# A three-stage token kernel on one core: the first block's filter matrix is fetched another way, the last block's arithmetic is dealt out to other engines, and the planner's table is new

## The chip, the cores and the metric

The program runs on 1 core of a Trainium2 chip. The core has TensorE (PE, matrix products into PSUM), VectorE (DVE), ScalarE (ACT), GpSimd (POOL, which here works on SBUF tiles alone) and SyncE (SP, which here only issues DMAs). The metric is the device time of one execution in microseconds; lower is better.

## The reference, cut to what matters

Everything is float32. 8192 tokens (2 sequences of 4096) of 192 numbers pass through three stages, and the last result is the output.

```
w   = softmax(weight, axis=-1)                     # 8 heads x 7 taps
out = einsum('hk,bskhg->bshg', w, windows(x, 7))   # causal: 6 zero rows ahead of a sequence, 24 channels a head
h   = out @ moe_w_in ; g = maximum(0.01 * h, h)    # 192 -> 2048
y   = g @ moe_w_out                                # 2048 -> 192
h   = y @ moe2_w_in
P   = a0 + a1*h + a2*h^2 + a3*h^3
Q   = 1 + |b0|*|h| + |b1|*h^2
z   = (P / (Q + 1e-6)) @ moe2_w_out
```

The four weight matrices arrive as 64-bit floats, so the kernel reads them as pairs of 32-bit words and turns them into float32 itself.

## The kernel before, in words

**Blocks and groups.** The tokens are cut into 16 blocks of 512. The 2048 hidden columns are cut into 16 groups of 128 (`j`). For one layer, block and group, PE runs `gemm1` (five matmuls of 128x512 into one PSUM bank), other engines make the activation `g` from it, split it into a rounded part `gH` and a remainder `gL`, and PE runs `gemm2_hi` (three matmuls with `gH`) and `gemm2_lo` (two with `gL`), which add into two accumulator banks. The three-part products carry float32 accuracy through a faster matmul format.

**Per group of layer 2.** ACT makes `p1 = a3*h + a2` and `|b1|*|h|` (`l2_vp`, two instructions); DVE makes `D = (|b1||h| + |b0|)*h` (`l2_D`); ACT takes its absolute value (`l2_abs`), then `1/sqrt(D + 1)` and its square (`l2_rs`, `l2_R`), and `D + 1` (`l2_Q`, on ACT or POOL as the planner picks). DVE makes the polynomial (`l2_p2`, `l2_p3`) and `gH` (`l2_hi`). POOL multiplies `Q * gH` (`l2_w`), DVE takes the remainder (`l2_r`), POOL multiplies it by `R` into `gL` (`l2_lo`). That is five DVE instructions, six or seven of ACT and two or three of POOL for ten matmuls. Layer 1 needs one of DVE, two of ACT and one of POOL per group.

**The first stage.** The causal filter is a matmul: the taps of a head stand along the diagonals of a 109x103 band matrix, the moving operand holds the rows of `x` in chunks of 103 tokens, and PE's result is copied by ACT (`conv_evac`) to `xc`, transposed by PE (`trans`) and split by ACT and DVE (`x_hi`, `x_lo`). To make the band, the softmaxed taps are put into a DRAM scratch (`s_put`, ACT's queue), read back twice with a stride of one element a partition (`s_get`, ACT's queue, 256 KB each), and turned round in the free dimension by DVE (first half) and ACT (second half) (`s_band`).

**The start.** Weights come in pieces (`raw` buffers, three of them) on SP's queue. A piece is made into float32 by two ACT and four DVE instructions (`cv_abs`, `cv_low`, `cv_clip`, `cv_bits`) and split (`w_hi` ACT, `w_lo` DVE or POOL). A piece of kind `r` is first copied to both partition halves by DMA (`r_dup`). PE runs 11 matmuls without use ahead of the first filter (`s_warm`) and one after the filter and one after the transposes (`s_fill`).

**What sets the order.** `Planner.run` lays out all groups of instructions before the program is built. Each has a rank (a base plus `OFF[name]`) and an estimated duration; among those whose inputs are there and which lie within `WINDOW` of the lowest rank and among the first `LOOK` of an engine, it takes the one with the least start plus `PULL * rank`. Each engine then runs its instructions strictly in that order, so one that waits holds all behind it. Layer 2 of a block is interleaved with layer 1 of the block two further on; only the end of the program has layer 2 alone. In the profile L234 is any ACT arithmetic, L237 and L240 the two-input forms on DVE or POOL, L243 a matmul, L474 a transpose of `trans`, L323 `s_get`, L329 `s_band` on DVE, L411 `r_dup`, L619 the stores of the output.

## Time and profile before

| | us |
|---|---|
| median of 3 runs (lowest, highest) | 1282.11 (1279.03, 1282.89) |
| the profiled execution | 1279.76 |
| its span in the trace | 1278.0 |
| PE busy in the span | 1238.8 (97%) |
| ACT, DVE, POOL busy | 1183.0, 1171.2, 1145.9 |

The span begins with the first instruction and ends with the last; 1.76 us of the execution lie outside it. Four engines are busy 90% of it or more, so an average tells little. The page's 40 slices show where that is not so: the first slice and the last two. The rest of the reading goes by stretches.

### The profile page before, as it was taken

The page shows a single profiled execution, that of the slowest core. Times are in us where ns is not written, and L with a number is a line of the kernel's source. Part 1 is how long each engine was busy: PE and PEld are TensorE (multiplying, and loading weights), DVE is VectorE, ACT ScalarE, POOL GpSimd, SP SyncE. Part 2 cuts the span into 40 slices and gives each one's busy share as a digit, 9 for nine tenths or more (in the row PEclk, how much of TensorE's full clock was granted, in tenths as well). Part 3 has the DMA queues.
Part 4 walks back from the last instruction along what each step waited for, and adds up shares of the span by engine and source line. Part 5 has one row for each costly group of instructions (what it writes and reads, how often), then busy time and mean ns, then how long its engine had stood idle before and what let it go on. Part 6 is the DMA issues. An engine that isn't in the chain of part 4 may idle for free.

```text
span 1278.0 us, 17949 instructions
## 1 busy us (share of the span) xinstructions
PE 1238.8 (97%) x5562; PEld 1005.1 (79%) x5562; DVE 1171.2 (92%) x1797; ACT 1183.0 (93%) x2193; POOL 1145.9 (90%) x922
## 2 busy tenths in 40 slices
PE   7999999999999999999999999999999999999975
PEld 5777878888888788887878878788888888888753
DVE  5999989999998989989899999999999989999997
ACT  5999999999999999999989999999999999999995
POOL 1896999999999899998989899999999999989886
PEclk8999999999999999999999999999999999999998
DMA  6551001010010101000000101001010100000000
GB/s 180 140 176 57 1 1 28 1 29 1 1 28 1 27 1 28 1 8 21 1 13 1 28 1 20 9 1 28 1 28 1 29 1 7 7 1 13 1 13 13
DMA packets 70140, 30.21 MB, mean 24 GB/s; under 512 B 52518, under 2 KB 67484, under 8 KB 70044
## 3 DMA queue, kind: packets, MB, share of 16 engines
q1 hardware_dynamic: 68956, 28.54, 9.0%
q8 instruction: 43, 0.70, 0.2%
q10 hardware_dynamic: 1088, 0.53, 0.1%
q14 instruction: 53, 0.43, 0.1%
HBM read 20.67 MB, written 6.30 MB: 21 GB/s over the span
## 4 chain that ended last, share of the span: by engine, by line
PE 75%; DVE 12%; ACT 8%; issue 2%; POOL 1%; DMA 1%; ACTq 0%; DVEq 0%; POOLq 0%
PE bank L243 39%; PE acc L243 36%; ACT work L234 4%; DVE work L237 2%; DVE work L240 2%; DVE bank L240 2%; ACT raw L234 2%; DVE pair L240 2%; DVE raw L240 1%; DVE xl L237 1%; ACT pair L234 1%; PE bank L474 1%; ACT xh L234 1%; POOL pair L237 1%; DVE bank L376 1%
## 5 line engine op out<-in xcount | busy, mean ns | idle before, releaser
L243 PE MATMUL acc<-pair,wo 128*128 128x512 f32 x2560 | 655.9, 393 | 7.7 <-POOL pair L237 6.9
L243 PEld LDWEIGHTS acc<-pair,wo 128*128 128x128 f32 x2560 | 478.8, 189 | 110.0 <-POOL pair L237 10.1
L234 ACT ACTIVATE work<-work 128x512 f32<-128x512 f32 x550 | 339.2, 634 | 23.0 <-DVE work L240 18.9
L237 POOL TENSOR_TENSOR pair<-work,pair 128x512 fp32r<-128x512 f32 x192 | 249.8, 1303 | 29.2 <-ACT pair L234 26.7
L237 DVE TENSOR_TENSOR work<-work,bank 128x512 f32<-128x512 f32 x364 | 243.5, 678 | 7.2 <-ACT work L234 6.5
L237 POOL TENSOR_TENSOR work<-work,pair 128x512 f32<-128x512 f32 x156 | 202.4, 1297 | 37.2 <-DVE pair L240 20.2
L243 PE MATMUL bank<-xh,wiH 128*128 128x512 f32 x512 | 208.2, 407 | 16.5 <-DVE work L240 6.4
L234 ACT ACTIVATE work<-bank 128x512 f32<-128x512 f32 x348 | 205.0, 595 | 8.5 <-PE bank L243 6.8
L243 PE MATMUL bank<-xh,wiL 128*128 128x512 f32 x512 | 200.5, 392 | 1.2 <-POOL wiL L237 1.2
L243 PE MATMUL bank<-xh,wiR 128*128 128x512 f32 x512 | 200.3, 391 | 0.3 <-DVE wiR L237 0.3
L243 PE MATMUL bank<-xl,wiH 128*128 128x512 f32 x512 | 200.2, 391 | 0.0
L243 PE MATMUL bank<-xl,wiR 128*128 128x512 f32 x512 | 200.0, 391 | 0.0
L234 ACT ACTIVATE raw<-raw 128x512 f32<-128x512 f32 x242 | 149.4, 633 | 9.5 <-DVE raw L240 8.4
L237 POOL TENSOR_TENSOR raw<-raw,pair 128x512 f32<-128x512 f32 x100 | 130.3, 1303 | 21.0 <-DVE pair L240 13.1
L240 DVE SCALAR_TENSOR_TENSOR pair<-bank,a_sb,work 128x512 fp32r<-128x512 f32 x192 | 142.7, 743 | 6.3 <-PE acc L243 2.5
L237 POOL TENSOR_TENSOR pair<-work,work 128x512 fp32r<-128x512 f32 x112 | 145.5, 1301 | 3.2 <-DVE work L240 2.3
L243 PEld LDWEIGHTS bank<-xh,wiH 128*128 128x128 f32 x512 | 96.3, 188 | 58.9 <-DVE work L240 15.7
L240 DVE SCALAR_TENSOR_TENSOR work<-work,b_sb,bank 128x512 f32<-128x512 f32 x156 | 115.4, 740 | 18.0 <-ACT work L234 16.8
L240 DVE SCALAR_TENSOR_TENSOR bank<-work,a_sb,bank 128x512 f32<-128x512 f32 x172 | 128.8, 749 | 2.1
L240 DVE SCALAR_TENSOR_TENSOR work<-bank,a_sb,work 128x512 f32<-128x512 f32 x156 | 116.3, 745 | 14.4 <-POOL work L237 13.3
L234 ACT ACTIVATE pair<-work 128x512 fp32r<-128x512 f32 x192 | 121.3, 633 | 2.2 <-DVE work L237 1.5
L234 ACT ACTIVATE work<-bank,a_sb 128x512 f32<-128x512 f32 x172 | 117.3, 682 | 4.3 <-PE bank L243 2.4
(81 smaller groups left out, 1896.9 us busy)
## 6 DMA issues: line engine op xcount, KB each, us to landing
raw<-in_moe_w_out_dram SPq DMA_DIRECT2D x16, 384.0 KB, 3.2
xt<-in_x_dram SPq DMA_DIRECT2D x14, 384.0 KB, 3.6
out_dram<-work SPq DMA_DIRECT2D x80, 64.0 KB, 1.9
raw<-in_moe_w_in_dram SPq DMA_DIRECT2D x8, 512.0 KB
raw<-in_moe_w_in_dram SPq DMA_DIRECT2D x8, 256.0 KB, 4.4
work<-work SPq DMA_DIRECT2D x16, 128.0 KB, 2.7
xt<-in_x_dram SPq DMA_DIRECT2D x18, 72.0 KB, 3.8
out_dram<-raw SPq DMA_DIRECT2D x16, 64.0 KB, 2.8
```

Source lines behind the costliest of these rows:

```text
L234: nc.scalar.activation(out=out_, in_=in_, func=func, **k)
L237: (eng or nc.vector).tensor_tensor(out=out_, in0=in0, in1=in1, op=op)
L240: nc.vector.scalar_tensor_tensor(out=out_, in0=in0, scalar=s, in1=in1, op0=op0, op1=op1)
L243: nc.tensor.matmul(out=out_, lhsT=w, rhs=r, start=start, stop=stop)
L376: nc.vector.tensor_scalar(out=a, in0=a, scalar1=F64_TINY, scalar2=F64_HUGE, op0=ALU.max, op1=ALU.min)
L474: nc.tensor.transpose(ps[:, t * CT:t * CT + k], xc[0:k, t, m * P:(m + 1) * P], ident[0:k, 0:k])
```

## The change

- The band is read back straight into its tile, both halves on SP's queue, and nobody turns it round (`s_get`; `s_band` is gone). The filter's results of a chunk therefore come out with the tokens reversed; `trans` writes the chunks from the back of its bank, so that a whole block is reversed, and `x_hi` and `x_lo` of layer 1 read the bank backwards. The last chunk of a block is loaded with 109 rows instead of 106, and the stationary operand is the last 103 columns of the band.
- SP reads the small vectors `a`, `b` after the band, and the third weight piece (`w_out`) only once the first is converted.
- For the first block the wrapped columns of `xc` are copied by DVE (`conv_wrap`) instead of ACT.
- PE gets 13 useless matmuls at the start instead of 11, one more behind the first block's `x_lo`, and four that wait for the first `w_out` piece (`FEED0`).
- In the last block, groups 2, 5, 8 and 11 make `D` without DVE: ACT takes `|h|` and `|b1|*|h|+|b0|` and POOL multiplies them (`l2_up`, `l2_t`, `l2_ut`). The planner may put `l2_lo` of groups 14 and 15 and `l2_w` of group 15 on DVE. `gemm2_hi` of groups 13 to 15 may come before their `gemm2_lo`s, which come last, together; four useless matmuls (`FEED`) wait for tiles of groups 13 to 15. Three of the six last stores go out on ACT's queue.
- The planner's numbers differ: `GAP`, `PREP`, `WINDOW`, `LOOK`, `REST`, `FIN`, `CV2`, `CV3` and 14 entries of `OFF`.

```diff
-PREP = 27.404
-WARM = 11
+PREP = 26.968
+WARM = 13
-WINDOW = 27.767
-LOOK = 19
+WINDOW = 39.292
+LOOK = 28
-CV1, CV2, CV3 = 9.735, 23.683, 5.167
+CV1, CV2, CV3 = 9.735, 28.752, 4.82
+FEED0 = ((('xl', 0, 0, 0), 1), (('wH', 0, 'o', 0), 2), (('wL', 0, 'o', 0), 2))
+GPDEN = (2, 5, 8, 11)
+ENDW = (15,)
+EARLY = (13, 14, 15)
+FEED = (('gH', 13), ('h', 14), ('h', 15), ('gH', 15))
+ENDV = (14, 15)
...
     def s_get(eng, m):
-        nc.scalar.dma_start(out=buf[("rev", m)].rearrange("p (h j) -> p h j", h=HB), in_=src)
-    def s_band(eng, m): ...
+        nc.sync.dma_start(out=band[:, m * HB:(m + 1) * HB, :], in_=src)
...
-            mm(pv[:, :, hh * G:(hh + 1) * G], band[0:CR, h, 0:CT],
+            mm(pv[:, :, hh * G:(hh + 1) * G], band[0:CR, h, P - CT:P],
...
+    def conv_wrap(eng, i):
+        pv = conv_view(buf[("cps", i, 1)], blocks[i][2])
+        nc.vector.tensor_copy(out=xc[:, 0:pv.shape[1], D:D + R], in_=pv[:, :, HC - R:HC])
...
-            nc.tensor.transpose(ps[:, t * CT:t * CT + k], xc[0:k, t, m * P:(m + 1) * P], ident[0:k, 0:k])
+            c1 = n - t * CT
+            nc.tensor.transpose(ps[:, c1 - k:c1], xc[0:k, t, m * P:(m + 1) * P], ident[0:k, 0:k])
...
+    def l2_up(eng, i, j):
+        l2_p1(eng, i, j)
+        act(b("D", 1, i, j), b("h", 1, i, j), ACTF.Abs)
+    def l2_t(eng, i, j):
+        act(b("R", 1, i, j), b("D", 1, i, j), scale=regs["b1"], bias=b_sb[:, 0:1])
+    def l2_ut(eng, i, j):
+        d = b("D", 1, i, j)
+        tt(d, d, b("R", 1, i, j), ALU.mult, nc.gpsimd)
...
-            nc.sync.dma_start(out=dst, in_=src)
+            (nc.scalar if eng == "ACT" else nc.sync).dma_start(out=dst, in_=src)
...
-            src = lambda k=xps: buf[k]
+            src = lambda k=xps, n=n: buf[k][:, 0:n][:, ::-1]
...
+            end = DVE(t_dve(n)) if i == NB - 1 and j in ENDV else []
+            endw = DVE(t_dve(n)) if i == NB - 1 and j in ENDW else []
-            on(POOL(t_pool(n)), s, 10.6, l2_lo, i, j, r=[dk, rk], w=[gl], take=("pair", gl))
+            on(POOL(t_pool(n)) + end, s, 10.6, l2_lo, i, j, r=[dk, rk], w=[gl], take=("pair", gl))
+            early = i == NB - 1 and j in EARLY
+            on(PE(t_pe(n, 3)), s, 15.36 - 9.0 * early, gemm2_hi, *k, r=wk + [gh], ...)
+            last.append((s, k, wk, gl, ak))
+            if not early or j == NJ - 1:
+                for s, k, wk, gl, ak in last:
+                    on(PE(t_pe(n, 2)), s, 15.37, gemm2_lo, *k, r=wk + [gl], w=ak)
+                del last[:]
+        if i == NB - 1:
+            for t, j in FEED:
+                on(PE(0.3), s, 9.0, s_fill, 1, r=["ident", (t, 1, i, j)], w=[("acc", 0, 1)])
```

How the rows of three engines move, first ACT at the start of the program (`bank0` and `work3` or `work1` belong to the first weight piece, `raw1` is the second, `xc` the filtered first block, `wiR` and `wiH` are parts of the first layer's weights, `xh` its input). Before:

```order
L318 DMA taps_dram<-work0_103 8x256
L323 DMA work1_104<-taps_dram 128x4x128
L323 DMA work2_105<-taps_dram 128x4x128
L234 ACTIVATE bank0_99<-raw0_126 128x512
L234 ACTIVATE work3_106<-raw0_126 128x512
L234 ACTIVATE band_62<-work2_105 128x512
L234 ACTIVATE bank2_101<-raw1_127 128x512
L234 ACTIVATE xc_78<-bank1_100 103x5x96
```

And after the change:

```order
L324 DMA taps_dram<-work0_103 8x256
L240 ACTIVATE bank0_99<-raw0_126 128x512
L240 ACTIVATE work1_104<-raw0_126 128x512
L240 ACTIVATE bank1_100<-raw1_127 128x512
L240 ACTIVATE work3_106<-raw1_127 128x512
L240 ACTIVATE xc_78<-bank2_101 103x5x96
L240 ACTIVATE xc_78<-bank3_102 103x5x96
L240 ACTIVATE wiR0_72<-work2_105 128x512
L240 ACTIVATE wiH0_68<-work3_106 128x512
L240 ACTIVATE xh000_79<-bank0_99 128x512
```

The band copy between the first and the second piece is gone, both conversions of the second piece stand ahead of the filter's copies, and the first `wiR` part, which needs `r_dup`, now stands ahead of `xh`.

SP's queue in the same place, before and then after (`raw1` and `raw2` are the second and third weight piece, `a_sb` and `b_sb` the small vectors, `work` <- `work` is `r_dup`):

```order
L353 DMA raw1_127<-in_moe_w_in_dram 128x1024
L298 DMA a_sb_65<-in_moe2_a_dram 128x4
L299 DMA b_sb_66<-in_moe2_b_dram 128x2
L359 DMA raw2_128<-in_moe_w_out_dram 128x2x384
L411 DMA work4_107<-work3_106 64x512 x2
L411 DMA work6_109<-work3_106 64x512 x2
```

```order
L351 DMA raw1_127<-in_moe_w_in_dram 128x1024
L329 DMA band_62<-taps_dram 128x4x128 x2
L304 DMA a_sb_65<-in_moe2_a_dram 128x4
L305 DMA b_sb_66<-in_moe2_b_dram 128x2
L409 DMA work2_105<-work1_104 64x512 x2
L357 DMA raw2_128<-in_moe_w_out_dram 128x2x384
L409 DMA work4_107<-work1_104 64x512 x2
```

The band's two reads stand right behind the second weight piece, and `w_out` has moved behind the first half of `r_dup`.

DVE at the end of the program, before and then after (`bank1` is group 15's `h`; `pair2_118`, then `pair5_121`, its `gH`; `work0` or `work1` with `acc11` is the final add):

```order
L240 SCALAR_TENSOR_TENSOR bank1_100<-work7_110,a_sb_65,bank1_100 128x512
L240 SCALAR_TENSOR_TENSOR pair2_118<-bank1_100,a_sb_65,work8_111 128x512
L240 SCALAR_TENSOR_TENSOR raw2_128<-bank0_99,a_sb_65,raw2_128 128x512
L240 SCALAR_TENSOR_TENSOR raw2_128<-bank1_100,a_sb_65,raw2_128 128x512
L598 STREAM_TRANSPOSE work1_104<-acc10_97 128x512
```

```order
L246 SCALAR_TENSOR_TENSOR bank1_100<-raw1_127,a_sb_65,bank1_100 128x512
L246 SCALAR_TENSOR_TENSOR pair5_121<-bank1_100,a_sb_65,raw0_126 128x512
L246 SCALAR_TENSOR_TENSOR work5_108<-bank3_102,a_sb_65,work5_108 128x512
L243 TENSOR_TENSOR raw2_128<-raw2_128,pair5_121 128x512
L246 SCALAR_TENSOR_TENSOR raw2_128<-bank1_100,a_sb_65,raw2_128 128x512
L243 TENSOR_TENSOR pair8_124<-raw2_128,raw0_126 128x512
L611 STREAM_TRANSPOSE work10_113<-acc10_97 128x512
```

Behind the last `gH` DVE now runs `l2_w` and `l2_lo` of group 15 itself, before and after group 15's `l2_r`; group 14's `l2_lo` stayed on POOL.

## Rows read from the trace of the kernel before

**Rows 1.** The page's 40 slices: tenths of each slice that the engine was busy.

```profile
PE   7999999999999999999999999999999999999975
PEclk8999999999999999999999999999999999999998
```

**Rows 2.** Windows: us, busy (instructions) of PE, PEld, DVE, ACT, POOL; clock; DMA share; GB/s.

```profile
20.76:31.80 11.04, 9.86 (x45) 8.08 (x45) 7.59 (x16) 6.79 (x14) 2.56 (x2) 0.69 0.64 191
140.00:400.00 260.00, 259.75 (x1195) 213.49 (x1194) 239.02 (x363) 245.86 (x455) 246.68 (x195) 1.00 0.05 11
1206.09:1264.30 58.21, 43.79 (x164) 29.93 (x162) 57.43 (x90) 55.32 (x101) 46.48 (x37) 0.97 0.04 7
1264.30:1278.00 13.70, 5.57 (x12) 3.64 (x12) 4.50 (x7) 0.59 (x2) 5.37 (x5) 0.63 0.17 29
```

**Rows 3.** PE from 40 to 1200 us: a group's idle time and releasers; the longest wait.

```profile
L243 PE MATMUL bank<-xh,wiH 128*128 128x512 f32 x487 | 196.1, 403 | 6.7 <-DVE raw L237 3.0 <-DVE work L237 1.6 <-DVE work L240 1.1
...
PE bank L243 <- DVE raw L237: 3.0, 3, 1.3
```

**Rows 4.** Timeline of the start: start, duration, engine, line, tiles, count [idle before <- releaser].

```profile
2.39 7.88 PE L243 MATMUL acc<-qc,ident 128*128 128x256 f32 x22 [2.39 <-POOL ident masks.py:199]
...
6.80 1.01 ACTq L323 DMA_DIRECT2D work<-taps_dram  x2
...
9.26 0.70 DVE L377 TENSOR_SCALAR bank<-bank 128x512 int32<-128x512 int32 x1
12.68 0.43 DVE L329 COPY band<-work 128x512 f32<-128x512 f32 x1 [2.72 <-DMA work<-taps_dram]
13.02 0.69 DVE L240 SCALAR_TENSOR_TENSOR bank<-raw,bank 128x512 int32<-128x512 int32 x1
...
13.16 2.02 PE L243 MATMUL bank<-xt,band 109*103 109x120 f32 x16 [2.88 <-DVE band L329]
13.43 0.63 ACT L234 ACTIVATE band<-work 128x512 f32<-128x512 f32 x1 [4.35 <-DMA work<-taps_dram]
...
14.53 2.41 SPq L411 DMA_DIRECT2D work<-work  x4
...
20.76 0.50 PE L243 MATMUL bank<-xh,wiL 128*128 128x512 f32 x1 [1.15 <-POOL wiL L237]
...
25.26 3.50 PE L243 MATMUL bank<-xt,band 109*103 109x120 f32 x16 [1.19 <-DVE bank L240]
```

**Rows 5.** DMA packets by queue, 9.5 to 12.5 us: packets, MB, share of 16 engines.

```profile
q10 hardware_dynamic: 805, 0.40, 45.0%
q1 hardware_dynamic: 289, 0.38, 36.7%
```

**Rows 6.** Timeline of the end, as rows 4.

```profile
1264.79 0.75 DVE L240 SCALAR_TENSOR_TENSOR pair<-bank,a_sb,work 128x512 fp32r<-128x512 f32 x1
1265.45 0.74 DVE L240 SCALAR_TENSOR_TENSOR raw<-bank,a_sb,raw 128x512 f32<-128x512 f32 x1
...
1266.02 5.57 PE L243 MATMUL acc<-pair,wo 128*128 128x512 f32 x12 [3.59 <-POOL pair L237]
1267.16 2.51 POOL L237 TENSOR_TENSOR pair<-raw,work 128x512 fp32r<-128x512 f32 x2
1267.24 0.75 DVE L240 SCALAR_TENSOR_TENSOR raw<-bank,a_sb,raw 128x512 f32<-128x512 f32 x1 [1.04 <-POOL raw L237]
...
1272.37 3.01 SPq L619 DMA_DIRECT2D out_dram<-work  x6
1272.94 0.70 DVE L611 STREAM_TRANSPOSE work<-work 64x512 f32<-64x512 f32 x1
```

**Rows 7.** DVE's `x_lo` by source, 130 to 1190 us: duration ns least/median/most.

```profile
L237 DVE TENSOR_TENSOR xl<-bank,xh x26: 645/684/693, 158.1 to 1115.9; 128x512 fp32r<-128x512 f32 x26
L237 DVE TENSOR_TENSOR xl<-work,xh x11: 692/885/1664, 187.2 to 1132.0; 128x512 fp32r<-128x512 f32 x11
```

**Rows 8.** The page's costliest group of ACT: busy us, mean ns | idle before.

```profile
L234 ACT ACTIVATE work<-work 128x512 f32<-128x512 f32 x550 | 339.2, 634 | 23.0 <-DVE work L240 18.9
```

More of the change, by code (lines that the diff above doesn't have):

```diff
@@ L20 @@
 LEAD = 85.211
-GAP = 12.894
-PREP = 27.404
-WARM = 11
+GAP = 12.901
+PREP = 26.968
+WARM = 13
 WIDE = 256
@@ L679, in conv_leaky_rational_kernel @@
     on(DVE(0.7), -80, 0, s_norm, r=["wsm", "taps"], w=["taps"])
-    on(ACT(0.4), -82, 0, s_put, r=["taps"], w=["tdram"], extra=1.45)
+    on(ACT(0.4), -82, 0, s_put, r=["taps"], w=["tdram"], extra=2.4)
     for m in range(2):
-        on(ACT(0.35), -82, 0.1, s_get, m, r=["tdram"], w=[("rev", m)], take=("work", ("rev", m)), extra=DMA_LAND)
-    on(DVE(0.4), -84, 0, s_band, 0, r=[("rev", 0)], w=[("band", 0)])
-    on(ACT(0.52), -84, 0, s_band, 1, r=[("rev", 1)], w=[("band", 1)])
+        on(SP(0, 1), -82, 0.1, s_get, m, r=["tdram"], w=[("band", m)], extra=3.3)
+    on(SP(0, 2), -60, 0, s_small, r=["tdram"], w=["ab"], extra=DMA_LAND)
     on(PE(0.6 * WARM), -74, 0, s_warm, r=["ident", "qc"], w=[("acc", 0, 1)])
@@ L774, in layer2 @@
         n = blocks[i][2]
+        last = []
         for j in range(NJ):
@@ L779, in layer2 @@
             on(PE(t_pe(n, 5)), s, 1.08, gemm1, *k, r=x_keys(1, i) + w1_keys(1, j), w=[h], take=("bank", h))
-            on(ACT(t_act(n) + t_act(n, ptr=1)), s, 3.40, l2_vp, i, j, r=[h, "regs"], w=[dk, pk],
+            alt = i == NB - 1 and j in GPDEN
+            on(ACT(t_act(n) + t_act(n, ptr=1)), s, 3.40, l2_up if alt else l2_vp, i, j, r=[h, "regs"], w=[dk, pk],
                take=[("work", dk), ("work", pk)])
-            on(DVE(t_dve(n, 1)), s, 4.00, l2_D, i, j, r=[h, dk], w=[dk])
-            on(ACT(t_act(n, True)), s, 4.90, l2_abs, i, j, r=[dk], w=[dk])
+            if alt:
+                on(ACT(t_act(n, True, 1)), s, 3.9, l2_t, i, j, r=[dk, "regs"], w=[rk], take=("work", rk))
+                on(POOL(t_pool(n)), s, 4.5, l2_ut, i, j, r=[dk, rk], w=[dk])
+            else:
+                on(DVE(t_dve(n, 1)), s, 4.00, l2_D, i, j, r=[h, dk], w=[dk])
+                on(ACT(t_act(n, True)), s, 4.90, l2_abs, i, j, r=[dk], w=[dk])
             on(DVE(t_dve(n)), s, 4.91, l2_p2, i, j, r=[pk, h], w=[pk])
-            on(ACT(t_act(n, True)), s, 5.60, l2_rs, i, j, r=[dk], w=[rk], take=("work", rk))
+            on(ACT(t_act(n, True)), s, 5.60, l2_rs, i, j, r=[dk], w=[rk],
+               take=() if alt else ("work", rk))
             on(DVE(t_dve(n, 1)), s, 5.80, l2_p3, i, j, r=[pk, h], w=[h])
@@ L816, in conv_leaky_rational_kernel @@
         convert(n)
+    for k, count in FEED0:
+        on(PE(0.45 * count), 0, 4.0, s_fill, count, r=["ident", k], w=[("acc", 0, 1)])
     for i in range(2):
```

37 lines of the change are left out of this document (15 added, 22 removed).

## The prediction

> **What bounds the kernel now.** I read the slices first, then PE's waits, then both ends in order of time. The slices [rows 1] show PE busy nine tenths or more, with the clock at its upper level (2.4 GHz), everywhere but in the first slice and the last two. The stretch from 140 to 400 us says the same: PE 259.75 of 260.00 us [rows 2]. From 40 to 1200 us PE idles 6.7 us ahead of a group's first matmul, at most 1.3 us at once [rows 3]. So in the middle PE sets the time. The change leaves its work there as it is, and what there is to win lies at the ends.
>
> At the start the chain of waits goes through the band. Its reads are issued at 6.80; DVE and ACT, which run in order, stand still for it, 2.72 and 4.35 us, and DVE ends its copy so that PE can begin the filter at 13.16 [rows 4]. Behind DVE's copy is held the conversion of the first weight piece: its second clip ended at 9.96 (9.26 + 0.70), its next step began at 13.02. On that hang `r_dup` at 14.53, the first full group on PE at 20.76 and, at the end of a nearly unbroken DVE chain, the second block's filter at 25.26 [rows 4]. From there PE is busy without a pause, but first at the lower clock: 20.76 to 31.80 has a mean of 0.69 [rows 2], and 16 filter passes take 3.50 us at 25.26 against 2.02 at 13.16 [rows 4].
>
> At the end, from the last input of block 15 on, DVE is busy 57.43 of 58.21 us, ACT 55.32, PE 43.79 and POOL 46.48 [rows 2]. DVE is the bound there, with ACT 2.1 us behind it. Then comes a chain: the last `gH` (begun at 1264.79, over when the next DVE instruction starts at 1265.45), `l2_w` on POOL, `l2_r` on DVE at 1267.24, two `l2_lo`s on POOL until 1269.67. PE meanwhile runs its last 12 matmuls in 5.57 us, until 1271.59 [rows 6]; the clock of 0.63 in that stretch [rows 2] says that most of it is at 1.2 GHz. Two transposes and an add, and six stores on one queue, end the program.
>
> **The start, step by step.** Without the copy, DVE's step at 13.02 can begin at 9.96: 3.06 us earlier, and `r_dup` with it (about 11.5). ACT's 4.35 us of waiting go too, so the second piece is converted ahead of the filter. The filter itself waits for the later of two things. One is the band. From 9.5 to 12.5 us its 805 packets took 45.0% of 16 engines [rows 5], which is 3 x 16 x 0.45 / 805 = 27 ns each; the two halves (1024 packets of 512 bytes) need 1.7 us of all engines alone. Now they share with `w_out` (36.7%), which will stand behind them. Issued at 6.80 as before, they can't land before 8.5, and with `w_out` away not after 12.68; I take 11.0, since the second weight piece is still being moved at 6.80. The other is the longer warm-up: 22 passes end at 10.27 (mean 0.36 us), four more end by 11.7 at that mean. So the filter begins near 11.2 instead of 13.16, which is early enough for the DVE chain.
>
> A rule speaks against the new queue. The Trainium skill (DMA: Bandwidth & Descriptors, Queues, rings and completion order) says that a DMA engine takes turns between the queues that have work, but takes one queue's in order. By it the band loses its turns against the second weight piece, whereas the trace shows ACT's queue (q10) and SP's (q1) being served side by side; no row tells what it costs, and by it at its worst the filter begins at 12.7, the start gives 1.5 instead of the 3.0 below, and the sum is 1274.3.
>
> Against the 3.06 us stand a DVE copy for the wrapped columns (like the 0.43 us copy that goes: nothing net) and five more useless matmuls ahead of the second block's filter, ten passes. At full clock PE's steady work needs 260.00 / 1195 = 0.22 us a matmul [rows 2], mostly of 512 columns in one pass; a filler's pass can't be dearer by much, so about 2 us, of which the first two passes lie in a wait for `x_lo`. What they can give back is the 3.50 - 2.02 = 1.5 us of the second filter. I count these against each other and take **3.0 us** for the start. Bounds: 0, if the clock falls all the same and the ten passes take the warm-up's 0.36 each on the path; 4.5, if all 3.06 and 1.5 come and the passes hide.
>
> **The last block.** Four `l2_D` leave DVE, each the 0.66 of its kind (1264.79 to 1265.45 [rows 6]): 2.64 us. ACT's count stays the same (`l2_up` and `l2_t` replace `l2_vp` and `l2_abs`), POOL gets 4 x 1.26 (2.51 / 2 [rows 6]) = 5.0 us, which its 11.7 us of idle time (58.21 - 46.48) hide; they would cost what they are if POOL came to hold `l2_rs`, which now waits for it. But ACT has only 58.21 - 55.32 = 2.89 us to give before it is the bound itself. Between 0 and 2.64 I take **2.0**.
>
> **The last chain.** From the last `gH`, 1265.45, to PE's end, 1271.59, are 6.14 us. After it: `l2_r` of group 14 0.66, `l2_w`, `l2_r` 0.66, `l2_lo`, then about 0.2 to PE and two matmuls, 0.22 and the whole 0.40 of a last one [rows 3]. Group 15's `gH` products are done by then, and the four fillers lie in PE's 14 us of idle time (58.21 - 43.79 [rows 2]); they cost nothing unless the tile they wait for holds up a product behind them. The two multiplications are new on DVE; both inputs lie in SBUF. The nearest rows are `x_lo`: with one input in PSUM 0.684 and never over 0.693, with both in SBUF 0.885 in the median and up to 1.664 [rows 7]. I take 1.0 each, since POOL will be at work beside them. That is 3.3 + 0.8 = 4.1: **2.0 us** less. Bounds: 0.69 each gives 2.7, 1.66 each with PE's matmuls at the 0.46 of rows 6 (5.57 / 12) 0.3. POOL's own last product comes sooner: group 14's `gH` is three DVE instructions (2.0 us) ahead of group 15's, and `l2_w` and two `l2_lo`s take 3.8.
>
> A rule speaks against this step as well. The Trainium skill (GPSIMD Engine Reference, Specifications) says that POOL shares its SBUF interfaces with DVE and they disturb each other where a DVE instruction has two SBUF inputs. The trace agrees, 1.664 against 0.693 at most. By that rule at its worst the two instructions eat 1.3 of the 2.0 us.
>
> **The stores.** Six on one queue run from 1272.37 to 1275.38; the last result is there at 1273.64 (1272.94 + 0.70 [rows 6]). On two queues the last can be issued by 1274.2, 1.2 us sooner. The packets share the same 16 engines, so I take **0.8**; bounds 0 and 1.2.
>
> **What costs nothing.** Reversed reading of PSUM: ACT's reversed band copy took 0.63 [rows 4], and a normal instruction of that size from SBUF takes 0.634 [rows 8]; for DVE no row shows it, and it could cost from nothing up to 16 x 2 x 0.68 = 22 us of DVE's time if it ran at half speed, most of it inside DVE's 21 us idle per 260 [rows 2]. Three more rows in a load of 109: nothing, 25 us ahead. The later `w_out`: issued behind the first half of `r_dup`, near 12.5 instead of about 7, it is wanted by ACT and DVE behind the first block's `x_lo`, near 17.5, so 5 us hide its way; were it later, the fillers that wait for it would hold PE (b). `a` and `b`: not wanted before layer 2. The new order in the middle: PE's idle time is 6.7 us; it may win that at most or lose as much, and I take 0.
>
> **Sum.** 3.0 + 2.0 + 2.0 + 0.8 = 7.8. From the profiled 1279.76 that gives 1272.0. This execution lies 2.35 under the median of the runs and near the lowest; I go up a third of that: **1272.8 us**.
>
> **Rivals.** (a) *ACT and POOL hold the end.* If ACT becomes the bound at once and the two SBUF products are slow, the end gives 0 + 0.3 + 0.8 instead of 4.8: 1276.5. For it: ACT is only 2.1 us behind DVE. Against: it has 2.89 us idle. Chance 0.14. (b) *The start gives nothing*, because PE's clock falls as it does now (0.69) and the fillers run at 0.36 a pass ahead of the second filter: 1275.8. For it: the fillers wait for `w_out`, which comes later now. Against: the filter and the first groups move closer together. Chance 0.13; both together 1279.5, 0.03. (c) *A stall at every block boundary.* The rank table is new in the whole program; if `x_lo` of each next block comes late, be it by reversed reading, PE waits at 15 boundaries. Rows 3 show such waits singly, up to 1.3 us. At 1.0 each 1287.8; it turns the result slower from (7.8 + 3.8) / 15 = 0.8 us on. Against: now no boundary after 140 us costs more than its share of 6.7. Chance 0.06. (d) *More than counted*: the waits of the middle go as well, 1267. Chance 0.06.
>
> **How the numbers follow.** The forecast has 0.58, and its own range is 1269 to 1277. 0.3% of 1282.11 is 3.8 us, about what can be told from no change. Below 1278.3 lie nearly all of the forecast (0.56), most of (a) and (b) (0.11 and 0.10) and (d): 0.83. Slower is (c) alone, 0.05; the rest, 0.12, is no change. The range 1267 to 1279 leaves out (c), the edge of (d) and a few hundredths.
>
> **What would show it.** Start: DVE without a wait between 9.3 and 13, `r_dup` near 11.5, the filter near 11.2, the second group of matmuls near 17.5, the second filter's 16 passes in about 2.0. End: from the last `x_lo` to the last `gH` 2 us less than now (59.4), ACT over 97% busy; PE done about 4.1 after it; last store issued 1.2 sooner after PE's end. It is wrong if PE's idle time between 40 and 1200 differs from 6.7 by more than 3, or if the second filter starts no earlier than 24.

## The result, and the profile after

The changed kernel takes 1268.61 us in the median of 4 runs (1267.46 to 1269.48), the kernel before 1281.44 beside it (1279.03 to 1282.89): a ratio of 0.9901, 95% interval 0.9883 to 0.9919. The forecast was 1272.8, range 1267 to 1279. The profiled execution took 1268.59 us, 11.17 less than that of before; its span is 1266.8. Against a forecast sum of 7.8, the gain is larger, and a good part of it does not lie where it was put.

I divide both traces at four points. M is the moment at which PE has done the same useful matmuls (72, useless ones not counted): after, where its first `gemm2` begins (26.26); before, at 31.86, behind its first five. Then come the start of block 15's last `x_lo`, the stretch from that one's end (0.61 us on) to the end of the last `gH` (the last block), to PE's last matmul (the last chain), and to the span's end (the span is given to 0.1 us).

| us | M | M to last x_lo | last block | last chain | rest | span |
|---|---|---|---|---|---|---|
| before | 31.86 | 1173.62 | 59.36 | 6.14 | 6.41 | 1278.0 |
| after | 26.26 | 1171.42 | 59.13 | 3.82 | 5.56 | 1266.8 |
| gained | 5.60 | 2.20 | 0.23 | 2.32 | 0.85 | 11.2 |
| forecast | 3.0 | 0 | 2.0 | 2.0 | 0.8 | 7.8 |

The page's slices after, in tenths:

```profile
PE   8999999999999999999999999999999999999977
PEclk9999999999999999999999999999999999999988
```

Against [rows 1], the first slice has risen by one in PE and in the clock. The windows that answer to [rows 2] (busy us and instructions of PE, PEld, DVE, ACT, POOL; clock; DMA):

```profile
140.00:400.00 260.00, 260.00 (x1195) 214.37 (x1194) 241.52 (x366) 247.41 (x461) 242.73 (x192) 1.00 0.05 11
...
1198.29:1257.42 59.13, 47.69 (x171) 34.57 (x170) 56.71 (x87) 55.13 (x101) 52.53 (x42) 0.88 0.04 7
```

And the last block of before, up to the end of its last `gH`:

```profile
1206.09:1265.45 59.36, 43.79 (x164) 29.93 (x162) 58.45 (x91) 55.33 (x101) 47.63 (x38) 0.96 0.04 7
```

In the last block DVE has four instructions fewer, but is idle for 2.42 us now, where it was for 0.91; ACT is busy 93%, not over 97%; and PE's mean clock is 0.88, where it was 0.96. PE's waits from 40 to 1200 us, as [rows 3]:

```profile
L249 PE MATMUL bank<-xh,wiH 128*128 128x512 f32 x489 | 196.6, 402 | 6.7 <-DVE work L243 1.9 <-DVE work L246 1.8 <-DVE raw L243 1.7
```

6.7 us as before: what the middle won does not show as idle time. The start, as [rows 4]:

```profile
5.83 0.62 ACT L240 ACTIVATE bank<-raw 128x512 f32<-128x512 f32 x1 [2.98 <-DMA raw<-in_moe_w_in_dram]
...
6.66 0.94 SPq L329 DMA_DIRECT2D band<-taps_dram  x2
...
8.75 0.69 DVE L246 SCALAR_TENSOR_TENSOR work<-bank,work 128x512 int32<-128x512 int32 x1
...
9.47 1.14 SPq L409 DMA_DIRECT2D work<-work  x2
...
11.00 1.86 PE L249 MATMUL bank<-xt,band 109*103 109x120 f32 x16
...
15.92 0.50 PE L249 MATMUL bank<-xh,wiL 128*128 128x512 f32 x1
...
19.22 1.89 PE L249 MATMUL acc<-qc,ident 128*128 128x256 f32 x8
22.30 2.13 PE L249 MATMUL bank<-xt,band 109*103 109x120 f32 x16 [1.20 <-DVE work L243]
```

The filter begins at 11.00 with no wait for the band; `r_dup` goes out at 9.47, two us sooner than forecast, because ACT began its first conversion at 5.83. Before, ACT issued the band's reads itself at 6.80 [rows 4]. That issue waits for the write of the taps, and ACT's conversion, next in its order, began at 7.86, when the issue was over (e4 tries this). The trace of before doesn't say so: it gives ACT's wait to the weight piece.

```profile
7.86 0.64 ACT L234 ACTIVATE bank<-raw 128x512 f32<-128x512 f32 x1 [5.01 <-DMA raw<-in_moe_w_in_dram]
```

That piece was issued at 0.73 in both, and in the changed kernel it had landed by 5.83. The second filter runs at the upper clock now. The end, as [rows 6]:

```profile
1257.42 0.74 DVE L246 SCALAR_TENSOR_TENSOR work<-bank,a_sb,work 128x512 f32<-128x512 f32 x1
1258.08 0.68 DVE L243 TENSOR_TENSOR raw<-raw,pair 128x512 f32<-128x512 f32 x1
1258.31 1.60 POOL L243 TENSOR_TENSOR pair<-work,work 128x512 fp32r<-128x512 f32 x1 [0.33 <-DVE work L246]
1258.80 0.75 DVE L246 SCALAR_TENSOR_TENSOR raw<-bank,a_sb,raw 128x512 f32<-128x512 f32 x1
1259.65 0.80 DVE L243 TENSOR_TENSOR pair<-raw,raw 128x512 fp32r<-128x512 f32 x1
...
1259.96 1.28 PE L249 MATMUL acc<-pair,wo 128*128 128x512 f32 x4 [0.40 <-POOL pair L243]
...
1262.03 1.62 SPq L632 DMA_DIRECT2D out_dram<-work  x3
1262.03 1.68 ACTq L632 DMA_DIRECT2D out_dram<-work  x3
```

The two products on DVE take 0.68 and 0.80 us; POOL's beside them takes 1.60 instead of 1.26. PE has four matmuls left behind it, and ends at 1261.24.

### The profile page after: what moved, and what is told of

It reads as the page before. It is cut to its first block, busy times and chain, and to the rows that moved or that the text cites. A ratio compares the mean times of both kernels' runs of the same rounds, so it can differ in the third digit from the quotient of the medians.

```text
span 1266.8 us, 17977 instructions
## 1 busy us (share of the span) xinstructions
PE 1238.6 (98%) x5584; PEld 1009.1 (80%) x5584; DVE 1174.1 (93%) x1792; ACT 1180.7 (93%) x2194; POOL 1146.5 (91%) x924
## 4 chain that ended last, share of the span: by engine, by line
PE 71%; DVE 12%; ACT 11%; issue 3%; POOL 2%; DMA 1%; POOLq 0%; DVEq 0%; SPq 0%; ACTq 0%
PE bank L249 37%; PE acc L249 34%; ACT work L240 5%; DVE work L246 2%; ACT raw L240 2%; DVE work L243 2%; DVE pair L246 1%; DVE bank L246 1%; DVE xl L243 1%; ACT pair L240 1%; ACT xh L240 1%; POOL pair L243 1%; DVE raw L243 1%; PE bank L476 1%; DVE raw L246 1%
## 5 line engine op out<-in xcount | busy, mean ns | idle before, releaser
L240 ACT ACTIVATE work<-work 128x512 f32<-128x512 f32 x541 | 332.1, 632 | 21.6 <-DVE work L246 18.8
L243 DVE TENSOR_TENSOR work<-work,bank 128x512 f32<-128x512 f32 x376 | 251.2, 679 | 5.1 <-ACT work L240 4.0
L249 PE MATMUL bank<-xh,wiH 128*128 128x512 f32 x512 | 207.6, 405 | 12.5 <-DVE work L246 5.5
L240 ACT ACTIVATE raw<-raw 128x512 f32<-128x512 f32 x253 | 158.1, 634 | 10.5 <-DVE raw L246 8.8
L246 DVE SCALAR_TENSOR_TENSOR pair<-bank,a_sb,work 128x512 fp32r<-128x512 f32 x186 | 138.4, 744 | 7.8 <-ACT work L240 2.5
L246 DVE SCALAR_TENSOR_TENSOR bank<-work,a_sb,bank 128x512 f32<-128x512 f32 x183 | 137.3, 750 | 2.9
L243 POOL TENSOR_TENSOR raw<-raw,pair 128x512 f32<-128x512 f32 x98 | 127.4, 1300 | 12.3 <-DVE pair L246 4.0
L240 ACT ACTIVATE work<-bank,a_sb 128x512 f32<-128x512 f32 x183 | 125.1, 684 | 9.4 <-PE bank L249 8.4
```

Of the source, the lines that this page charges most:

```text
L240: nc.scalar.activation(out=out_, in_=in_, func=func, **k)
L243: (eng or nc.vector).tensor_tensor(out=out_, in0=in0, in1=in1, op=op)
L246: nc.vector.scalar_tensor_tensor(out=out_, in0=in0, scalar=s, in1=in1, op0=op0, op1=op1)
L249: nc.tensor.matmul(out=out_, lhsT=w, rhs=r, start=start, stop=stop)
```

## The experiments

Each edit is made on the changed kernel unless it says otherwise; the kernel before ran beside each (medians 1282.47, 1282.54, 1283.37 and 1282.5 in the four series). Of the kernels that start from the changed one, only e1's first series and e7 have a ratio to before whose interval lies clear of both of the changed kernel's (0.9883 to 0.9919, and 0.988 to 0.9906); for the others the length of the stretches in one execution each carries the reading. This table divides all traces as above; two rows with the same program show what one execution says.

| us | median | M | M to last x_lo | last block | last chain | rest |
|---|---|---|---|---|---|---|
| changed, again | 1268.24 | 27.47 | 1171.68 | 58.41 | 3.81 | 5.52 |
| e1 / again | 1273.33 / 1273.41 | 27.00 / 26.96 | 1171.19 / 1171.50 | 59.40 / 61.96 | 4.92 / 4.52 | 5.58 / 5.55 |
| e2 | 1270.81 | 28.46 | 1171.23 | 59.18 | 5.06 | 5.56 |
| e3 | 1271.16 | 27.57 | 1171.26 | 58.41 | 3.82 | 5.53 |
| e4 | 1271.61 | 29.54 | 1171.85 | 58.52 | 3.81 | 5.87 |
| e6 | 1270.52 | 27.29 | 1171.38 | 58.70 | 5.34 | 6.38 |
| e7 | 1274.38 | 30.34 | 1173.51 | 58.67 | 3.83 | 5.55 |
| e9 | 1267.97 | 26.04 | 1172.08 | 58.70 | 3.82 | 5.55 |
| e5 (before + numbers) | 1279.5 | 32.58 | 1171.91 | 60.95 | 5.31 | 6.34 |
| e10 (before + four D) | 1282.39 | 32.30 | 1176.03 | 57.97 | 7.21 | 6.38 |
| before, again | 1282.79 | 32.61 | 1175.94 | 59.37 | 6.21 | 6.36 |

**e1: all D of the last block on DVE again.**

```diff
-GPDEN = (2, 5, 8, 11)
+GPDEN = ()
```

> The changed kernel, with all sixteen D of the last block made on DVE again (GPDEN empty); nothing else is undone. In the trace after the change the stretch from block 15's last x_lo to its last gH took 59.13 us against 59.36 before, so four D fewer on DVE seem to have bought 0.2 us and not 2.0. Theory A (ACT holds DVE up in that stretch: DVE waited 1.7 us for ACT there, 0.3 before): with the four D back on DVE, its busy time grows by about 2 us and its waits for ACT shrink by about 1.5, the stretch is 59.3 to 60.2 long, the whole time is 0.2 to 1.0 us over that of the changed kernel. Rival B (the four D are worth the 2.0 that was forecast, and something else of the change in this stretch, such as the matmuls without use or the new order, costs 1.8): the stretch is 61 or more, the time 2.0 to 2.6 us longer. Rival C (POOL's four products delay l2_rs and cost more than they save): the stretch is shorter than 59.0, the time 0.3 to 1 us shorter.

Ratio to before 0.9934 (0.9921 to 0.9948): 5 us over the changed kernel, more than any theory said, while its trace shows 1.9 more span: the block as A expected (59.40), and 1.1 in the last chain, where the planner had now put group 14's `l2_lo` on DVE too and group 15's `l2_w` back on POOL, so this run undoes a little more than the four D. The profiled execution was the fastest of the five, so the same program was profiled once more:

> The kernel with all sixteen D of the last block on DVE once more. Its five times had a median of 1273.33, but the execution that was profiled took 1270.44, and its trace shows 1.9 us against the changed kernel, not 4.7. Theory A (the difference lies in the start or at the end, in a clock that falls in most executions and did not in the one profiled): a profile at 1272 to 1275 shows the second filter at 3 us or more, or PE's last matmuls at a clock under 0.8. Rival B (the last block is sensitive to small shifts: with DVE at 58.45 of 59.40 us every delay counts): a profile at 1272 to 1275 shows the stretch from the last x_lo to the last gH at 61 or more. If the profile lies at 1270 to 1271 again, this stays open.

Rival B. The two executions run alike up to the output of block 14; then small waits of DVE, 2.1 us more in all, and 0.5 us more of busy time were never made good. PE's mean clock in the stretch was 0.97 in the first and 0.92 in the second. All that DVE waited for in the second:

```profile
DVE work L246 <- ACT work L240: 0.9, 1, 0.9
DVE work L611 <- PE acc L249: 0.8, 1, 0.8
DVE raw L246 <- POOL raw L243: 0.7, 1, 0.7
DVE raw L246 <- ACT raw L240: 0.4, 1, 0.4
```

With four D off DVE the stretch took 58.41 to 59.18 in all eight profiles of kernels that start from the changed one: DVE's new idle time may be what swallows such delays; no run shows that by itself.

**e2: the last two products on POOL.**

```diff
-ENDW = (15,)
-ENDV = (14, 15)
+ENDW = ()
+ENDV = ()
```

> The changed kernel, with the last two multiplications (l2_w and l2_lo of group 15) on POOL again (ENDW and ENDV empty); the order of all other instructions is the same. From the last gH to PE's end it took 3.82 us after the change and 6.14 before. Theory A (the two products on DVE are what shortened this chain): POOL has four products of 1.28 us behind the last gH, PE ends 5.5 to 6.2 us after it, the time is 1.7 to 2.4 us longer. Rival B (the two multiplications with both inputs in SBUF cost on DVE, beside POOL, nearly what they cost on POOL, and PE's clock and the matmuls moved ahead made the chain shorter): PE ends 3.8 to 4.6 us after the last gH, the time is less than 0.8 us longer.

Ratio 0.9907 (0.9892 to 0.9922), 2.2 to 2.6 us over the changed kernel's medians. The chain is 5.06: 1.24 us of the 2.32 are these two products, between A and B. Behind the last `gH` POOL now has two products more in a row:

```profile
1261.24 1.28 POOL L243 TENSOR_TENSOR pair<-work,work 128x512 fp32r<-128x512 f32 x1
...
1262.47 1.29 POOL L243 TENSOR_TENSOR pair<-raw,raw 128x512 fp32r<-128x512 f32 x1
...
1263.81 0.73 PE L249 MATMUL acc<-pair,wo 128*128 128x512 f32 x2 [0.50 <-POOL pair L243]
```

**e3: fewer useless matmuls at the start.**

```diff
-        for n in range(WARM):
+        for n in range(WARM - 2):
...
-        on(PE(0.45 * count), 0, 4.0, s_fill, count, ...
+        on(PE(0.45 * count), 0, 4.0, s_fill, 0, ...
```

> The changed kernel with 11 useless matmuls at the start instead of 13, and without the five of FEED0; the order of everything else is the same. In the trace after the change the granted clock is 1.00 from 2.40 us on and the second filter's 16 passes take 2.13 us; before, the clock was 0.69 from 20.76 to 31.80 and they took 3.50. Theory A (the extra matmuls keep the clock up between the transposes and the second filter): without them the clock falls to the lower level for several us around 16 to 28 us, the second filter takes 3 us or more, and the time is 1 to 4 us longer. Rival B (PE is busy enough by itself now that the first groups follow the transposes at once; the ten passes are on the path): clock 1.00 as with them, the second filter begins 1.5 to 2.2 us earlier, the time is 1 to 2.2 us shorter. Rival C (neither: the second filter waits for DVE's chain in any case, and the ten passes lay in that wait): within 0.8 us.

Ratio 0.9915 (0.9901 to 0.9928): 2.6 to 2.9 us longer, A's size, but not in A's place. PE runs dry for 2.00 us ahead of the first filter, and the lower clock comes there, not at the second filter:

```profile
10.80 1.04 PE L249 MATMUL bank<-xt,band 109*103 109x120 f32 x8 [2.00 <-issue]
12.02 1.92 PE L249 MATMUL bank<-xt,band 109*103 109x120 f32 x8 [0.18 <-DMA band<-taps_dram]
...
23.61 2.13 PE L249 MATMUL bank<-xt,band 109*103 109x120 f32 x16 [3.10 <-DVE work L243]
```

This execution was the fastest of its five (1269.0), so most of the 2.7 us are not in it; they stay unplaced. B falls: without the ten passes PE only waits longer for DVE.

**e4: the band's reads on ACT's queue.**

```diff
     def s_put(eng):
         nc.scalar.dma_start(out=taps_dram, ...)
+        for m in range(2): ...
+            nc.scalar.dma_start(out=band[:, m * HB:(m + 1) * HB, :], in_=src)
     def s_get(eng, m):
-        nc.sync.dma_start(out=band[:, m * HB:(m + 1) * HB, :], in_=src)
+        pass
```

> The changed kernel, with the two reads of the band issued on ACT's queue, right behind the write of the taps, as the kernel before issued them; the band still lands in its tile reversed and nobody copies it. SP's queue loses the two issues. Theory A (part of the start's gain, about 2 us, comes from ACT no longer standing still ahead of its first conversion: before, ACT issued the two reads from 6.80 to 7.81 and converted the first weight piece from 7.86; after, with the reads on SP, from 5.83): ACT's first conversion begins at 7.8 to 7.9 again, r_dup near 11.5 instead of 9.47, the second filter begins 1.5 to 2.2 us later than its 22.30, and the time is 1.5 to 2.2 us longer. Rival B (the later conversion is hidden, because the filter and the transposes set the first matmul at 15.25 and the weights are there in time): first conversion at 7.8 as well, but the second filter within 0.5 of 22.30 and the time within 0.6. Rival C (the band comes earlier on its own queue and the filter with it): shorter by up to 0.5, bounded by the useless matmuls, which end at 10.89.

Ratio 0.9915 (0.9902 to 0.9929), 3.0 to 3.4 us longer: A, with more than its 2. ACT's first conversion waits for its own queue again, the second filter is 1.85 us later, and in the longer gap ahead of it the clock falls:

```profile
6.61 0.98 ACTq L328 DMA_DIRECT2D band<-taps_dram  x2
...
7.63 0.63 ACT L240 ACTIVATE bank<-raw 128x512 f32<-128x512 f32 x1 [4.79 <-issue]
...
24.15 3.40 PE L249 MATMUL bank<-xt,band 109*103 109x120 f32 x16 [2.19 <-DVE work L243]
```

**The changed kernel again.**

> The changed kernel once more, on the chip of the next runs, to tell how far two profiled executions of one program lie apart, stretch by stretch: the kernel with only the last two products moved has the same instructions in the same order up to the end, and still reached block 15's last x_lo at 1200.38 where the changed kernel was at 1198.29. Theory A (2 us in the middle are no more than the spread from run to run, so that the 2.4 us that the middle seemed to win can't be told from nothing): the last x_lo between 1197 and 1201, the start (four matmuls of the first group 1 to 4, up to the first gemm2's end) within 0.5 of the first profile. Theory B (the middle is the same to within 0.5 in each run of one program, so the 2.4 us are a gain): the last x_lo within 0.5 of 1198.3. The median 1268 to 1271 by either.

Ratio 0.9893 (0.988 to 0.9906). Neither as written: the middle agrees to 0.3 us, the start differs by 1.2: PE waited 1.48 us ahead of the filter, for which the view names no releaser, and once more for the band's second half.

```profile
11.29 1.04 PE L249 MATMUL bank<-xt,band 109*103 109x120 f32 x8 [1.48 <-issue]
12.50 1.07 PE L249 MATMUL bank<-xt,band 109*103 109x120 f32 x8 [0.18 <-DMA band<-taps_dram]
...
23.51 2.13 PE L249 MATMUL bank<-xt,band 109*103 109x120 f32 x16 [1.70 <-DVE work L243]
```

Six executions with this start have M at 26.26 to 28.46, mean 27.24; the three of before at 31.86 to 32.61, mean 32.26. The start's gain is 5.0 us by these.

**e5: the kernel before with the new planner numbers alone.**

```diff
-GAP, PREP, WINDOW, LOOK, REST, OFF, FIN, CV2, CV3 = ...   # of before
+GAP, PREP, WINDOW, LOOK, REST, OFF, FIN, CV2, CV3 = ...   # of the changed kernel
```

> The kernel before, with nothing of the change but the planner's numbers (GAP, PREP, WINDOW, LOOK, REST, FIN, CV2, CV3 and OFF); band, start, last block and stores as before. Theory A (the numbers alone do nothing in the middle; the gain is the start's and the end's): PE's idle time from 40 to 1190 us stays 6 to 8 us, the second filter begins near 25 and takes 3.5, the time is within 2 us of the kernel before. Rival B (the numbers are a good part of the gain, by the start's order of conversions or the 2.4 us that the middle seemed to win): 3 to 6 us under before. Rival C (the numbers fit the changed kernel alone): 1 to 5 us over before.

The edit changes 12 entries of `OFF`, all that differ between the two kernels. Ratio 0.9975 (0.9965 to 0.9985): 3.0 us faster, B's lower end. The middle takes 1171.91, as in the changed kernel, and the start wins nothing. The last block loses: 60.95 against 59.36 and 59.37, with PE's mean clock at 0.92 there instead of 0.96, and ACT waiting 3.1 us for PE instead of 1.3 and 0.8. The last chain is 0.8 to 0.9 shorter.

**e6: PE's end and the stores as before.**

```diff
-EARLY = (13, 14, 15)
-FEED = (('gH', 13), ('h', 14), ('h', 15), ('gH', 15))
+EARLY = ()
+FEED = ()
...
-                on(ACT(0.45) if i == NB - 1 and q % 2 else SP(0, 1), ...
+                on(SP(0, 1), ...
```

> The changed kernel, with the end of PE's queue and the stores as before: no useless matmuls in groups 13 to 15, the products with gH no longer moved ahead of those with gL, six stores on SP's queue; DVE's and POOL's instructions are the same in the same order. Of the 2.3 us that the stretch from the last gH to PE's end lost, 1.2 came back with the two products on POOL. Theory A (the other 1.1 are PE's: after, it had four matmuls of 1.28 us in all left behind the last l2_lo and ran at full clock; before, twelve in 5.57 at 0.54): PE ends 4.6 to 5.3 us after the last gH instead of 3.82, at a clock of 0.5 to 0.8 in that stretch. Rival B (PE has time enough in either order, since it waits for DVE and POOL): within 0.3 of 3.82. For the stores, from PE's end to the span's end: 0.6 to 1.2 us more than 5.56 if the forecast of 0.8 was right; less than 0.3 more if the stores' packets, not their issue, set the end. The time is 0.6 to 2.7 us longer in all.

Ratio 0.9904 (0.9889 to 0.9918), 1.9 to 2.3 us longer. A, at the upper edge of its range: PE's last 17 matmuls are one stretch of work at the lower clock (first row: timeline; second: window from the last `gH` to PE's end, clock 0.59).

```profile
1256.01 7.31 PE L249 MATMUL acc<-pair,wo 128*128 128x512 f32 x17 [1.07 <-POOL pair L243]
```

```profile
1257.98:1263.32 5.34, 5.27 (x14) 3.41 (x12) 2.89 (x5) 0.19 (x1) 2.14 (x2) 0.59 0.00 0
```

The chain is 1.52 longer, the rest 0.82, the stores' forecast. The new order and the useless matmuls were undone together, so which of them keeps the clock up isn't shown.

**e7: w_out ahead of the band.**

```diff
-           r=[("cv", 0, "r", 0)] if n == 2 else (), w=[key], ...
+           r=(), w=[key], ...
```

> The changed kernel with w_out, the third weight piece, issued on SP's queue ahead of the band's two reads, where nothing holds it, and not behind the first half of r_dup (the order of instructions in the middle shifts a little with it). Theory A (one queue is served in order and the DMA engines are 0.8 busy from 2 to 11 us, so 384 KB ahead of the band cost it 1 to 1.7 us; the filter now begins as soon as the useless matmuls end, at 11.0, so there is no slack): the filter begins at 12.0 to 12.7, waiting for the band, and the second filter 0.5 to 1.5 us later than 22.30, the time 0.5 to 2.5 us longer. Rival B (w_out is moved while the queue waits for the taps' write, and r_dup and the second half come earlier for it): the filter within 0.3 of 11.0 and the second filter up to 1 us earlier, the time up to 1 us shorter. Rival C (the later w_out holds something: the useless matmuls behind the first groups wait for it): no change in the first filter, the second filter 0.5 to 1 earlier.

Ratio 0.9935 (0.9922 to 0.9947), 5.8 to 6.1 us longer: A's mechanism, well beyond its price. The second half of the filter waits for the band, the first begins behind 2.00 us of idle time for which the view names no releaser, and from 13 to 19 us the clock is at 0.50; M is 3.1 later than the mean of the six above, and 2.1 lie in the middle (1173.51), whose order shifted (PE's listed waits sum to 8.4 us there, in the changed kernel to 6.3).

```profile
11.91 1.27 PE L249 MATMUL bank<-xt,band 109*103 109x120 f32 x8 [2.00 <-issue]
13.53 1.90 PE L249 MATMUL bank<-xt,band 109*103 109x120 f32 x8 [0.35 <-DMA band<-taps_dram]
```

**e9: the second half of the first wiR taken later.**

```diff
-                c += 12.0 * half * (n == 0)
+                c += 30.0 * half * (n == 0)
```

> The changed kernel, with the second half of the first wiR (it is read from the second half of r_dup, and first needed by group 8) taken later: ACT converts w_out's first half ahead of it, and its remainder is made on POOL, not DVE; every queue and every other instruction is in the order of the changed kernel. In three profiles of the changed start ACT waited 0.16, 0.70 and 1.23 us for that half of r_dup, with w_out's conversion, the wo split and the first l1_max behind it, and DVE spent 0.69 on it; the second filter, which waits for that l1_max, began at 22.30, 23.51 and 23.08. Theory A (what sets the second filter is this chain through ACT and DVE, held by the transfer): DVE's first clip of w_out begins at 16.3 to 16.6 instead of 16.96 to 18.16, the second filter at 21.3 to 22.2, the first gemm2 at 25.2 to 26.3 instead of 26.26 to 28.46, and the time is 0.7 to 2 us shorter than the changed kernel's 1268.2 to 1268.6, the middle (first gemm2 to block 15's last x_lo, 1171.2 to 1171.9 in eight profiles) as before. Rival B (w_out itself lands no earlier, since it stands ahead of that half on the same queue and the DMA engines are all busy from 13 to 22 us): ACT waits for w_out in its place, less than 0.5 us gained. Rival C (the wiR half comes too late for group 8 now, or POOL's 1.28 us for it hold l1_lo): PE waits for wiR or gL within the first block, 0.5 to 2 us longer.

A in the trace, nearly: the clip at 16.69, the second filter at 22.05, after a wait of 0.47. In time it is 0.3 to 0.6 us under the changed kernel; its ratio to before, 0.988 (0.9864 to 0.9897), overlaps the other's, so the two can't be told apart.

```profile
16.69 0.56 DVE L374 TENSOR_SCALAR bank<-bank 128x384 f32<-128x384 f32 x1
...
22.05 2.13 PE L249 MATMUL bank<-xt,band 109*103 109x120 f32 x16 [0.47 <-DVE work L243]
```

**e10: the kernel before with four D off DVE, and nothing else.**

```diff
+            alt = i == NB - 1 and j in (2, 5, 8, 11)
+            if alt: ...     # l2_up, l2_t on ACT, l2_ut on POOL, as in the change
```

> The kernel before, with one part of the change alone: groups 2, 5, 8 and 11 of the last block make D without DVE (ACT takes |h| and |b1||h|+|b0|, POOL multiplies); band, start, planner's numbers, last products and stores as before. Theory A (with all sixteen on DVE, the stretch from the last x_lo to the last gH has no slack, and each delay in it, from PE's clock at the end of block 14 on, is added up: 59.40 and 61.96 in two profiles of one program; with four off, DVE can catch up, and the stretch is 58.4 to 59.2 in six profiles): 58.4 to 59.2 here as well, and the times 1.5 to 3.5 us under the kernel before. Rival B (the four D's are worth the 0.3 to 0.7 us between the profile of the kernel before, 59.36, and that of the changed one): 58.4 to 59.2, but the times less than 1 us under the kernel before. Rival C (without the rest of the change ACT or POOL hold DVE up in another place): the stretch over 59.4.

Ratio 1.0002 (0.9994 to 1.0011): rival B in time, for C's reason at a later place. The block shrinks by 1.40 to 57.97, more than any theory said, but the last chain grows by 1.07 (1.00 against the second profile of before): POOL, with four products more in the block, has four left behind the last `gH`, where it had three.

```profile
1267.14 1.27 POOL L238 TENSOR_TENSOR raw<-raw,pair 128x512 f32<-128x512 f32 x1 [0.42 <-DVE pair L241]
1268.37 1.27 POOL L238 TENSOR_TENSOR pair<-work,work 128x512 fp32r<-128x512 f32 x1
1269.59 2.51 POOL L238 TENSOR_TENSOR pair<-raw,work 128x512 fp32r<-128x512 f32 x2
```

**The kernel before again.**

> The kernel before once more, for a second profile. Its first one took 1279.76, among the lowest of the more than thirty times that were measured since (medians 1281.4 to 1283.4). Theory A (the first profile caught a quick passage through the last block): a profile at 1281 to 1284 shows the stretch from block 15's last x_lo to its last gH at 60.5 to 62.5 instead of 59.36, with waits of DVE for PE's results of block 14 and for POOL, while the start (band copy at 12.7, second filter at 25.3) and the middle (1173.6 from the point where the four engines' work stands as at 26.43 after the change) are within 0.7 of the first. Rival B (the spread is the start's: the band's transfer and the clock at the second filter): the stretch within 0.5 of 59.36, the second filter 1 to 3 us later or slower.

A falls: the last block is 59.37. The second filter is 1.60 later, as B has it, and M 0.75; and 2.3 us lie in the middle, which neither theory said, all of it at one stall of PE that the first profile does not have:

```profile
268.13 0.50 PE L243 MATMUL bank<-xh,wiH 128*128 128x512 f32 x1 [1.44 <-DVE work L237]
```

Behind that stall is one instruction: an `x_lo` of DVE that reads two SBUF tiles while POOL is at work. It took 0.79 us in the first profile, where POOL's product beside it took 1.77 instead of 1.31, and 3.29 in the second. The first profile, then the second:

```profile
261.09 0.79 DVE L237 TENSOR_TENSOR xl<-work,xh 128x512 fp32r<-128x512 f32 x1
261.27 1.77 POOL L237 TENSOR_TENSOR pair<-raw,work 128x512 fp32r<-128x512 f32 x1
```

```profile
261.61 3.29 DVE L237 TENSOR_TENSOR xl<-work,xh 128x512 fp32r<-128x512 f32 x1
```

e10, with the same middle (1176.03), has the same stall, behind an `x_lo` of 3.30. The ten profiles with the new numbers in their order (e7 shifts it) lie between 1171.19 and 1172.08. Against the commoner course of before, the middle's gain is 4.5 us and not 2.2, which fits the medians, 13 to 14 us apart, where the first pair of profiles is 11.2 apart.

## Why the prediction was right, and where it was not

**The start, 3.0; measured 5.6 in the first pair, 5.0 on the means.** The stall named was the right one: DVE goes on without a break at 9.3, the filter begins at 11.00 (forecast 11.2). The step that was short is "ACT's 4.35 us of waiting go too, so the second piece is converted ahead": it counted the wait behind the reads and not the wait in front of them. ACT's queue had held the *first* conversion by 2.03 us (5.83 against 7.86, the same weight piece), and with it `r_dup` (9.47, forecast 11.5) and the second group of matmuls (15.92, forecast 17.5). e4 puts only that back and loses 3 us; its M of 29.54 leaves 2.7 of the start's 5.0, near the 3.0 forecast. The clock's part came as counted in size, 2.13 for the second filter, forecast 2.0, against 3.50, but not by the useless passes behind the first groups: e3, without them, has 2.13 there too. They cost little, since PE still waits 1.20 for DVE behind them. On the queue, e7 agrees with the Trainium skill (DMA: Bandwidth & Descriptors, Queues, rings and completion order: one queue's work is done in order): with `w_out` in front the filter's second half is at 13.53. The worst case that the rule was weighed for, the filter at 12.7, did not come: the filter began at 11.00, and in the second profile at 11.29, its second half at 12.50.

**The last block, 2.0; measured 0.2.** The four D themselves were priced near enough: alone, in the kernel before, they shorten the block by 1.40, though POOL's four products more cost 1.0 of that again in the last chain (e10). What failed is that the sum let nothing else move there. The planner's new numbers, for which it had a term of 0 in the middle and none in this block, lengthen it by 1.6 (e5). All 14 profiles, by who makes D and by PE's mean clock in the block:

| D of the last block | PE's clock | ACT waits for PE, us | block, us |
|---|---|---|---|
| all on DVE: before, before again, e1 | 0.96 to 0.97 | 0.8 to 1.5 | 59.36 to 59.40 |
| all on DVE: e5, e1 again | 0.92 | 3.1, 4.0 | 60.95, 61.96 |
| four off DVE: e10 | 0.96 | 1.4 | 57.97 |
| four off DVE: the changed kernel twice, e2, e3, e4, e6, e7, e9 | 0.88 to 0.94 | 1.8 to 3.2 | 58.41 to 59.18 |

So with the clock as before the four D are worth 1.4 in the block; where it is lower, the two groups lie 1.8 to 3.6 apart. In the first pair DVE's busy time fell by 1.74 (58.45 to 56.71), but 1.5 us more of it went idle, 1.7 us of this waiting for ACT, which itself waited 3.0 us for PE. The longest of these waits stands in a stretch in which PE is busy throughout at the lower clock (first row: window; then ACT and DVE):

```profile
1208.00:1212.00 4.00, 4.00 (x10) 3.06 (x10) 3.35 (x6) 2.56 (x5) 3.95 (x4) 0.50 0.00 0
```

```profile
1210.99 0.69 ACT L240 ACTIVATE work<-bank,a_sb 128x512 f32<-128x512 f32 x1 [1.44 <-PE bank L249]
1212.20 0.75 DVE L246 SCALAR_TENSOR_TENSOR work<-work,b_sb,bank 128x512 f32<-128x512 f32 x1 [0.85 <-ACT work L240]
```

Such a stretch comes three times in the changed kernel's last block; in that of before once (mean 0.72 from 1215 to 1221), and again in its last 1.2 us, where PE has nothing to do. That the clock is what took the gain back is read from these traces; no run holds the clock up there, and within the last group of the table the block does not go by the clock alone. With the rest of the end as changed, putting the four D back costs 5 us in the medians (e1), about 1 of it in the last chain, where the planner chose otherwise.

**The last chain, 2.0; measured 2.3. The stores, 0.8; measured 0.85.** Right, and with the right price of a product beside POOL: 0.68 and 0.80 against the 1.0 taken. What the sum had only in passing is PE: e2 says 1.24 for the products, e6 1.52 for the order and the clock of PE's last matmuls (the two overlap), and the planner's numbers alone already give 0.8 (e5). The Trainium skill's rule on the shared interfaces (GPSIMD Engine Reference, Specifications) was borne out in e1, where such a product on DVE took 1.44 us beside POOL in both profiles; in the changed kernel the loss fell on POOL's (1.60). The bound of 1.66 was too low: one `x_lo` took 3.29 in the second profile of the kernel before, and 3.30 in e10.

**The middle, 0; measured 2.2, and 4.5 against the commoner course of before.** "It may win that at most or lose as much, and I take 0" held within its bounds of 6.7, but not in its reason: idle time is unchanged. e5 shows that the numbers alone do it. Which of them was not tried. The 2.3 us by which the two courses of before differ are one long `x_lo` beside POOL; why it is long in two profiles of three stays open.

**What costs nothing** held: reading PSUM backwards takes what it took forwards ([rows 7] has 645/684/693).

```profile
L243 DVE TENSOR_TENSOR xl<-bank,xh x26: 643/684/692, 152.7 to 1107.7; 128x512 fp32r<-128x512 f32 x26
```

None of the rivals came as written. (a) had DVE wait for ACT in the last block, which it did, but ACT itself waited for PE. The time is nearest (d)'s 1267, but PE's waits in the middle, which (d) names, did not go. So the range held partly by luck, by errors of opposite sign: 1.8 us too much for the last block, 2.6 and 2.2 too little for the start and the middle.

## What to carry to other kernels

A DMA issue that waits for data belongs on a queue whose engine has nothing else to do then: on an engine that computes, it holds the work behind it, and the trace may show that work as waiting for its own input; compare the start of that work with a sibling that isn't held. Work taken off the busiest engine is worth its busy time only as far as the results that it waits for come sooner too: here 2.64 us off DVE gave 1.4, and a new order of the same work took 1.6 back in the same stretch, so a new order needs a term of its own wherever it reaches. And before a profile is taken as the base of a sum, read a second one: here one long instruction in the middle, present in some executions only, was larger than three of the forecast's four terms.
